# A table of buffers and a new order for the first 1550 steps of an attention and gated FFN kernel

## The chip, the cores and the metric

The kernel runs on one NeuronCore of a Trainium2 chip. The metric is the device time of one execution in microseconds (us), from several runs of the same kernel; a profile of one execution shows where that time goes. The names of the engines in the profile are PE (TensorE, with PEld for its weight loads), DVE (VectorE), ACT (ScalarE), POOL (GpSimd) and SP (SyncE, which issues most transfers).

## The reference

```python
def _attn_ref(q, k, v):                       # 8 batches, 8 heads, 576 rows, 64 columns
    q_s = softmax of q over its 64 columns
    k_s = softmax of k over the 576 rows
    kv = np.einsum('bhsd,bhse->bhde', k_s, v)
    return np.einsum('bhsd,bhde->bhse', q_s, kv)

def _moe_ref(x, w_gate, w_val, w_out, rms_g): # x: 4608 rows of 512, 1536 hidden columns
    rms = np.sqrt(np.mean(x * x, axis=-1, keepdims=True) + 1e-06)
    xn = x / rms * rms_g
    g = xn @ w_gate
    silu = g * (1.0 / (1.0 + np.exp(-g)))
    val = xn @ w_val
    return silu * val @ w_out
```

The heads of the attention's output are laid side by side and go as `x` into the gated FFN. The weights come as 64-bit floats.

## The kernel before, in words

The 4608 rows are nine blocks `j` of 512. Blocks 0 to 2 (`JP = 3`) go through the FFN one after the other; the other six are taken in three pairs `p`, for which the multiplications are saved by Strassen's scheme. The hidden columns are twelve chunks of 128. A step `s` counts block and chunk together: step 13 is chunk 1 of block 1.

The work is written as small functions, one per step. `ORDER` is a text of 3337 steps, which a loop at the end of the kernel calls from first to last under a manual schedule, so each engine receives its instructions in the order in which the text names them. A letter behind a colon chooses the engine: `:A` ScalarE, `:D` VectorE, `:P` GpSimd, `:S` the queue of SyncE. An engine takes its instructions strictly in turn and waits at the first that isn't ready.

The steps that matter here:

- `constants` makes the identity and `mean_w` on GpSimd; `warm` multiplies `mean_w` by itself on TensorE as filler (49 multiplications in all).
- K and V of a batch and a pair of heads: `k_load`, `k_max0` or `k_max` (maximum, VectorE), `k_tr` (transpose, TensorE), `k_top` (maximum, VectorE), `k_rows` (back, TensorE), `k_sub` (VectorE), `k_exp` (ScalarE), `k_mm` (K times V, TensorE), then `k_eps`, `k_rec` and `kv_hi`, `kv_lo` or `kv_norm0` (the normed product, split in two parts). `v_load` and `v_ones` fill V and its column of ones; `kv_zero` and `kv_zero0` clear buffers.
- q of a block and a pair of heads: `q_load`, `q_max`, `q_sub`, `q_exp`, `q_sum`, `q_rec`, `q_mul`, a transpose (`q_t`; for blocks 0 and 1 `q_t0` on TensorE with its copy `q_c0`), `q_hi` and `q_lo`, `q_x` or `q_x0` (q times KV, TensorE). Names that end in 0 are for the first blocks.
- x of a block: `x_hi`, `x_lo`, `x_sq`, then the norm in `n_sum`, `n_t`, `n_y0`, `n_y1`, `n_rows`.
- Weights: `load_w`, `conv_mul`, `conv_shift`, `conv_low` and `conv_add` turn 64-bit floats into 32-bit ones; `w_hi`, `w_lo`, `o_hi` and `o_lo` split a chunk into a rounded part and what is left (`copy` at L409 and the subtraction at L922 and L930); `s_add`, `s_hi`, `s_lo` do it for sums of weights that the pairs need, and `b_hi`, `b_lo`, `t_add` for the pairs' x.
- FFN of a step: `f1.s.0` and `f1.s.1` (gate and value, twelve 512-column multiplications each, L1005), `g_mul`, `silu`, `h_mul`, `h_hi` and `h_lo` (L1026), `f2` (twelve more, L1042) and at the end of a block `store`. For the pairs `pp` and later `qq` are TensorE's products.

Buffers come from pools with a number of places each, taken in turn. The eight PSUM banks are three pools: two for the results of `f1` (`ps_gv`), four for those of `f2` (`ps_o`), and two for all else (`ps_a`). The pairs choose among the pools by the table `BANKS`. A step that takes a bank waits until the last reader of the bank's former content is done: in `ps_gv` that is `g_mul` or `h_mul` of the step before.

Of the kernel before, what the change touches and what calls it, by code (L numbers as in the profile page):

```python
# [28 lines left out]
q_exp.0.2 q_eps0.0.0:D k_mm.0.0 k_eps.0.0:D conv_shift.1.1 warm.2.23 q_rec0.0.1 q_mul0.0.1:P conv_low.0.1.1 k_load.1.0
load_w.0.2 warm.2.11 q_rec0.0.0 k_sub.0.3 k_exp.0.3 k_rec.0.0 warm.2.12 q_sum0.0.2 q_eps0.0.2:A k_rows.0.2 k_sub.0.2  # L30
q_load0.1.0 v_ones.0.3 k_mm.0.1 k_eps.0.1:A conv_mul.0.1 warm.2.21 q_sub0.0.3:D load_w.2.1 k_rec.0.1 warm.2.22
q_rec0.0.2 q_exp.0.3 load_w.1.0 warm.2.5 k_mm.0.3 q_mul0.0.0:P q_t0.0.0 conv_mul.0.0 q_load0.1.1 load_w.3.0 load_w.2.0
q_mul0.0.2:P kv_norm0.0.0:D k_exp.0.2 k_eps.0.3:A q_t0.0.1 conv_low.0.0.1 kv_norm0.0.1:D conv_shift.0.1 conv_add.0.1.1
conv_shift.0.0 load_w.4.1 load_w.1.2 q_c0.0.0:A kv_zero0.1 q_sum0.0.3 q_eps0.0.3:D warm.2.13 q_rec0.0.3 q_c0.0.1:A
q_load0.1.2 k_mm.0.2 k_eps.0.2:A conv_mul.0.2 q_x0.0.0 k_max.1.0 conv_add.0.0.1 k_rec.0.3 kv_norm0.0.3:D warm.2.24
load_w.4.0 w_hi.0.0.2:A x_sq.0.0 k_tr.1.0 q_mul0.0.3:D q_t0.0.3 load_w.3.2 q_c0.0.3:A q_x0.0.1 k_rec.0.2 q_max0.1.0
# [1450 lines left out]
```

## Time and profile before

| what | value |
|---|---|
| device time, median of 3 runs | 932.93 us (932.87 to 935.09) |
| span of the profiled execution | 930.7 us |
| TensorE busy | 920.5 us (99%) |
| VectorE busy | 727.0 us (78%) |
| GpSimd busy | 522.4 us (56%) |
| ScalarE busy | 461.4 us (50%) |

The span runs from the first to the last instruction of the profiled execution and is its own time in the profile; the device time has 2.2 us around it that hold no instruction. A busy share is the part of the span in which an engine worked. A multiplication's recorded end is modelled, and neighbours overlap, so the pace of TensorE is better read from how long a whole group of multiplications takes.

### The profile page before, as it was taken

How to read it: one execution, taken by the hardware profiler on the slowest of the kernel's cores; microseconds unless marked ns; L12 is line 12 of the kernel's file. 1: busy time of each engine (PE TensorE's matmuls, PEld its weight loads, DVE VectorE, ACT ScalarE, POOL GpSimd, SP SyncE). 2: the span in 40 equal slices, each digit the busy share in tenths (PEclk: the TensorE clock that was granted, in tenths of full speed). 3: DMA queues.
4: the chain of work that ended last, by engine and by line, in shares of the span. 5: the costliest groups of instructions: out<-in, count | busy, mean ns of one | idle time of the engine just before them, and what ended most of it. 6: DMA issues, size and time to landing. Idle time of an engine off the chain costs nothing.

```text
span 930.7 us, 14213 instructions
## 1 busy us (share of the span) xinstructions
PE 920.5 (99%) x4621; PEld 748.1 (80%) x4621; DVE 727.0 (78%) x1520; ACT 461.4 (50%) x741; POOL 522.4 (56%) x539
## 2 busy tenths in 40 slices
...
GB/s 266 281 268 195 161 90 252 316 275 323 244 221 188 257 246 244 253 255 210 246 211 204 240 274 277 280 304 284 202 184 182 210 195 285 267 185 181 69 158 91
DMA packets 216569, 211.06 MB, mean 227 GB/s; under 512 B 138416, under 2 KB 177840, under 8 KB 211888
## 3 DMA queue, kind: packets, MB, share of 16 engines
...
q14 instruction: 36, 0.29, 0.1%
...
## 4 chain that ended last, share of the span: by engine, by line
PE 95%; DVE 3%; DMA 1%; issue 0%; ACT 0%; POOL 0%; DVEq 0%; ACTq 0%; POOLq 0%
PE ps_gv L1005 20%; PE ps_gv L1154 18%; PE ps_o L1154 12%; PE ps_o L1042 10%; PE ps_a L1154 7%; PE ps_o L1363 6%; PE ps_o L1247 4%; PE ps_a L1363 4%; PE ps_gv L1363 3%; PE ps_a L594 2%; PE ps_a L802 2%; PE ps_a L1247 2%; PE ps_gv L1247 2%; PE ps_o L802 1%; PE ps_gv L476 1%; DMA wd<-w 1%
## 5 line engine op out<-in xcount | busy, mean ns | idle before, releaser
L1005 PE MATMUL ps_gv<-xh,w 128*128 128x512 f32 x576 | 190.6, 397 | 1.3 <-DVE gs L1017 1.3
L1154 PE MATMUL ps_gv<-x,ring 128*128 128x512 f32 x576 | 143.0, 392 | 0.0
L1005 PEld LDWEIGHTS ps_gv<-xh,w 128*128 128x128 f32 x576 | 108.2, 188 | 26.0 <-DVE gs L1017 1.4
L1154 PEld LDWEIGHTS ps_gv<-x,ring 128*128 128x128 f32 x576 | 107.0, 188 | 23.0
L1005 PE MATMUL ps_gv<-xl,w 128*128 128x512 f32 x288 | 112.3, 391 | 0.0
L1175 DVE TENSOR_TENSOR tmp<-tmp,ps_gv 128x512 f32<-128x512 f32 x84 | 57.3, 684 | 49.6 <-PE ps_gv L1154 48.1
L1154 PE MATMUL ps_o<-x,ring 128*128 128x512 f32 x360 | 85.1, 389 | 0.0
L1127 POOL DMA_DIRECT2D ring<-wd x54 | 31.0, 575 | 91.3 <-PE ps_o L1154 34.1
L1154 PEld LDWEIGHTS ps_o<-x,ring 128*128 128x128 f32 x360 | 67.6, 188 | 14.2
L1042 PE MATMUL ps_o<-o,hh 128*128 128x512 f32 x288 | 73.1, 396 | 0.0
L1005 PEld LDWEIGHTS ps_gv<-xl,w 128*128 128x128 f32 x288 | 54.2, 188 | 10.6 <-issue 0.4
L1042 PEld LDWEIGHTS ps_o<-o,hh 128*128 128x128 f32 x288 | 53.0, 188 | 11.3 <-issue 0.4
L1175 DVE TENSOR_TENSOR tmp<-tmp,ps_o 128x512 f32<-128x512 f32 x42 | 28.7, 685 | 29.1 <-PE ps_o L1154 26.0
L409 ACT CAST hh<-gs 128x512 fp32r<-128x512 f32 x48 | 29.6, 616 | 31.7 <-DVE gs L1017 17.4
L1127 POOL DMA_DIRECT2D w<-wd x18 | 10.1, 559 | 58.2 <-PE ps_a L1154 37.9
L922 POOL TENSOR_TENSOR w<-w,w 128x512 fp32r<-128x512 f32 x29 | 39.3, 1363 | 5.1 <-ACT w L409 5.0
L1042 PE MATMUL ps_o<-o,hl 128*128 128x512 f32 x144 | 38.7, 391 | 0.0
L1154 PE MATMUL ps_a<-x,w 128*128 128x512 f32 x144 | 36.9, 392 | 0.0
L541 DVE TENSOR_REDUCE cm<-kt 128x128 f32<-128x640 f32 x28 | 36.7, 1310 | 0.1
L1154 PE MATMUL ps_a<-x,ring 128*128 128x512 f32 x144 | 36.7, 390 | 0.0
L1026 POOL TENSOR_TENSOR hl<-gs,hh 128x512 fp32r<-128x512 f32 x21 | 28.2, 1343 | 14.9 <-ACT hh L409 9.0
L1154 PE MATMUL ps_gv<-x,w 128*128 128x512 f32 x144 | 35.1, 391 | 0.0
...
## 6 DMA issues: line engine op xcount, KB each, us to landing
...
```

What stands on the lines that cost most here:

```text
L409: (e.copy if e is nc.scalar else e.tensor_copy)(dst, src)
L541: nc.vector.tensor_reduce(out=cm, in_=kt_[b, g].rearrange("p h j d -> p h d j"), axis=AX.X, op=ALU.max)
L802: nc.tensor.matmul(px[:, c0:c1], lhsT=wt, rhs=mv[:, c0:c1], start=(i == 0), stop=(i == 2))
L922: on(nc.gpsimd).tensor_tensor(out=w[:, :, 1], in0=halves(CHUNK[s], a, 1)[:, 0], in1=w[:, :, 0].bitcast(F32), op=ALU.subtract)
L1005: nc.tensor.matmul(pd[s], lhsT=w[:, a, c // 2, m, c % 2 * P:c % 2 * P + P], rhs=X[j, c][x], start=(n == 1), stop=(n == 3 * NKT))
L1026: on(nc.gpsimd).tensor_tensor(out=hl, in0=g_[s], in1=h_[s][0].bitcast(F32), op=ALU.subtract)
L1042: nc.tensor.matmul(po[t], lhsT=a[:, t * P:(t + 1) * P], rhs=w, start=(i == 0 and n == 0), stop=(i == NF - 1 and n == len(terms) - 1))
L1127: nc.gpsimd.dma_start(t, src.rearrange("p a b f -> p (a b f)"))
L1154: nc.tensor.matmul(abc[p, i, m, b], lhsT=src[:, h, c * P:(c + 1) * P], rhs=operand(o, c, x), start=first and n == 0, stop=n == 5, skip_gro ...
L1175: nc.vector.tensor_tensor(out=dst, in0=ux[u + (src,)], in1=abc[u + (b,)], op=ALU.add)
L1247: nc.tensor.matmul(pa[p, t, k], lhsT=a[:, k * P:(k + 1) * P], rhs=w, start=(c == 0 and n == 0), stop=(c == NF - 1 and n == 2))
L1363: nc.tensor.matmul(qacc[p, b, x], lhsT=ws[l][x], rhs=h[m], start=first and i == 0 and n == 0, stop=i == NH - 1 and n == 2, skip_group_chec ...
```

## The change

`ORDER` has the same 3337 steps in another order. In the sequence that each engine receives, the last difference stands at about step 1550, just ahead of the first product of the pairs (`pp.0.0.0.1`); from there on each engine has the same sequence as before. 181 steps have another engine letter, nearly all of them ahead of that place. From VectorE to GpSimd go, after those that go the other way are taken off, `w_lo` nine times, `s_lo` five and `o_lo` four times; from GpSimd to VectorE `q_mul`, `q_lo` and `x_nm`; from ScalarE to VectorE `h_hi`, `s_hi`, `b_hi`, some of `kv_hi`, `x_cp` and `q_c0`; to ScalarE from VectorE `kv_norm0` and `k_eps`.

The pools give way to a table, `SLOT`. It has a line for each kind of buffer: the width, and one digit for each time that the buffer is taken, in order, which names the place. The eight PSUM banks become one set (`ps.ps`, 390 digits), so any step can take any bank. A kind with width 0 still allocates a tile under the named place; one with a width uses one fixed tile for each place.

```diff
 ORDER = """
-kv_zero.4 k_load.0.0 v_ones.0.0 kv_zero0.0 g_load constants warm.2.2 warm.2.4 warm.2.7 warm.2.6 v_ones.1.1 k_max0.0.0
-warm.2.3 k_load.0.2 k_tr.0.0 k_top.0.0 k_max0.0.2 k_load.0.1 warm.2.8 k_max0.0.1 k_tr.0.2 warm.2.0 k_load.0.3
-k_max0.0.3 q_load0.0.1 q_max0.0.1 q_sub0.0.1:P q_exp.0.1 warm.2.1 k_rows.0.0 k_tr.0.3 warm.2.20 k_top.0.3 q_load0.0.2
-q_max0.0.2 v_ones.1.0 k_sub.0.0 k_exp.0.0 q_load0.0.0 v_load.0.0 k_tr.0.1 k_top.0.1 warm.9 warm.2.10 q_load0.0.3
-load_w.1.1 q_sub0.0.2:P q_max0.0.0 q_sum0.0.1 v_load.0.1 load_w.0.1 k_top.0.2 v_load.0.3 k_rows.0.3 load_w.0.0
-v_load.0.2 q_eps0.0.1:A q_sub0.0.0:P q_exp.0.0 conv_mul.1.1 q_max0.0.3 k_rows.0.1 k_sub.0.1 q_sum0.0.0 k_exp.0.1
...
-o_keep.12:S k_tr.2.1 store.0.0:A q_max2.2.2 n_rows.1 q_sub.2.2:P store.0.2:A k_top.2.1 g_mul.12 k_rows.2.1 s_lo.1.1:P
-k_mm.2.0 q_exp.2.2 k_sub.2.1 w_keep.13:S w_hi.14.0.2:A r_keep.1 f1.13.0 k_eps.2.0 q_half2.2.1 s_add.1.4:P k_load.2.2
-k_exp.2.1 q_max.2.3 silu.12 k_rec.2.0 w_lo.14.0:P k_mm.2.1 v_ones.2.2 w_lo.14.1:D kv_hi.2.0:A q_half.2.3 s_add.2.1:P
-s_keep.1.1:S v_load.2.2 store.0.3:A h_mul.12 s_add.0.1:P g_mul.13 f1.13.1 h_hi.12:A q_sum.2.2 h_lo.12:P kv_lo.2.0
-q_half2.2.2 s_add.0.3:P q_max2.2.3 q_sum2.2.2 q_sum2.2.1 k_eps.2.1 q_rec.2.2 k_rec.2.1 v_ones.2.3 q_sub.2.3:D
...
+v_ones.0.3 constants k_load.0.2 kv_zero.0 k_load.0.0 kv_zero.7 q_load0.0.1 kv_zero0.0 warm.2.7 k_load.0.1 warm.2.2
+k_load.0.3 q_load0.0.0 warm.2.6 k_max0.0.2 warm.2.4 load_w.0.1 k_max0.0.0 q_load0.0.2 warm.2.1 q_max0.0.1 v_load.0.1
+k_tr.0.0 q_sub0.0.1:D k_tr.0.2 v_load.0.0 k_top.0.0 q_exp.0.1 warm.2.10 k_max0.0.1 warm.2.8 k_max0.0.3 q_load0.0.3
+warm.2.20 q_sum0.0.1 warm.2.12 k_tr.0.3 load_w.1.1 q_max0.0.0 q_eps0.0.1:A warm.2.0 q_rec0.0.1 k_rows.0.0 k_top.0.3
+warm.2.3 q_sub0.0.0:P k_sub.0.0 k_tr.0.1 v_load.0.2 k_rows.0.3 warm.9 v_ones.0.0 q_mul0.0.1:P v_load.0.3 k_top.0.1
+k_exp.0.0 q_max0.0.2 load_w.0.0 q_exp.0.0 k_sub.0.3 q_sub0.0.2:P k_load.1.0 k_rows.0.1 k_top.0.2 warm.2.23 kv_zero.4
+q_exp.0.2 k_sub.0.1 warm.2.11 k_rows.0.2 k_mm.0.0 k_sub.0.2 k_exp.0.1 load_w.0.2 q_max0.0.3 conv_mul.0.1 q_load0.1.0
+k_mm.0.1 k_exp.0.3 q_sum0.0.0 q_sub0.0.3:P q_eps0.0.0:A k_exp.0.2 q_rec0.0.0 q_sum0.0.2 warm.2.5 conv_low.0.1.1
...
+s_lo.1.1:D h_hi.11:A k_exp.2.0 q_sum.2.2 h_lo.11:P s_keep.1.1:S k_tr.2.1 f2.10 q_half.2.3 o_keep.13:S q_lo.2.0:P
+n_y0.1 o_keep.12:S n_y1.1 s_add.1.4:P f2.11 q_max2.2.3 s_hi.1.4:A q_rec.2.1 q_sub.2.3:P k_top.2.1 n_rows.1 g_mul.12
+s_lo.1.4:P store.0.0:A s_add.2.1:D k_mm.2.0 w_hi.14.0.2:A s_lo.1.2:P k_rows.2.1 k_load.2.2 f1.13.0 s_hi.2.1:A
+k_sub.2.1 k_eps.2.0:A w_lo.14.0:D k_exp.2.1 kv_lo.1.2:P k_rec.2.0 store.0.3:A q_half2.2.2 s_add.0.1:P kv_hi.2.0:D
+k_mm.2.1 g_mul.13 kv_lo.1.3:P f1.13.1 kv_lo.1.1:P v_load.2.2 kv_lo.2.0 silu.12 q_mul.2.1:P store.0.1:A h_mul.12
+silu.13 v_ones.2.2 h_hi.12:D w_lo.14.1:D h_lo.12:P k_max.2.2 r_keep.5 store.0.2:A f2.12 w_hi.15.0.2:A q_sum2.2.2
...
+SLOT = """
+ap.kt 0 001011010101001010101010110101100110011001
+ap.qt 512 01202102102120102102102102021210120120
+fp.gs 512 2011202121021012101211201010121110221201201201201201201201200120120
+ps.ps 512 651637314556012451502136373164551247421662304457310652360314725765762756765627652765625726572657527652752676272765262572675260541762305023503025230230250235023503253505023506124735607417142172142174174127421741241214142741247414217144271453604217141414274142714412474142714427141724172472172400656503506630536053654136027563065306530653065306531721724721720647253172472172427127427127417260
+small.rs 1 01221011100102220102202102102102
+wsp.w 0 0111010101101010101010101010101010
...
+"""
+class Slots:
+    def __init__(self, pool, key):
+        self.pool, self.take, self.width, self.fixed = pool, {}, {}, {}
+        for line in SLOT.split("\n")[1:-1]:
+            tag, *rest = line.split()
+            if tag.startswith(key + "."):
+                tag = tag[len(key) + 1:]
+                self.width[tag], self.take[tag] = int(rest[0]), iter(rest[1])
+    def tile(self, shape, dtype, name, tag=None, bufs=None):
+        tag = tag or name
+        if tag not in self.take:
+            return self.pool.tile(shape, dtype, name=name, tag=tag, **({} if bufs is None else {"bufs": bufs}))
+        key = f"{tag}_{next(self.take[tag])}"
+        if not self.width[tag]:
+            return self.pool.tile(shape, dtype, name=name, tag=key, bufs=1)
+        if key not in self.fixed:
+            self.fixed[key] = self.pool.tile([128, self.width[tag]], F32, name=key, tag=key, bufs=1)
+        n = 1
+        for x in shape[1:]:
+            n *= x
+        t = self.fixed[key][:shape[0], :n]
+        if dtype is not F32:
+            t = t.bitcast(dtype)
+        axes = "abcd"[:len(shape) - 1]
+        if len(axes) > 1:
+            t = t.rearrange(f"p ({' '.join(axes)}) -> p {' '.join(axes)}", **dict(zip(axes, shape[1:])))
+        return t
...
-    wsp = ctx.enter_context(tc.tile_pool(name="wsp", bufs=2))
+    wsp = Slots(ctx.enter_context(tc.tile_pool(name="wsp", bufs=2)), "wsp")
     big = ctx.enter_context(tc.tile_pool(name="big", bufs=1))
-    xp = ctx.enter_context(tc.tile_pool(name="xp", bufs=8))
-    fp = ctx.enter_context(tc.tile_pool(name="fp", bufs=3))
-    ap = ctx.enter_context(tc.tile_pool(name="ap", bufs=2))
+    xp = Slots(ctx.enter_context(tc.tile_pool(name="xp", bufs=8)), "xp")
+    fp = Slots(ctx.enter_context(tc.tile_pool(name="fp", bufs=3)), "fp")
+    ap = Slots(ctx.enter_context(tc.tile_pool(name="ap", bufs=2)), "ap")
     kvp = ctx.enter_context(tc.tile_pool(name="kvp", bufs=8))
-    small = ctx.enter_context(tc.tile_pool(name="small", bufs=3))
-    ps_gv = ctx.enter_context(tc.tile_pool(name="ps_gv", bufs=NGV, space=PSUM))
-    ps_o = ctx.enter_context(tc.tile_pool(name="ps_o", bufs=T, space=PSUM))
-    ps_a = ctx.enter_context(tc.tile_pool(name="ps_a", bufs=8 - T - NGV, space=PSUM))
-    pools = {"a": ps_a, "v": ps_gv, "o": ps_o}
-    attn_pool = ["a"]
+    small = Slots(ctx.enter_context(tc.tile_pool(name="small", bufs=3)), "small")
+    psum = Slots(ctx.enter_context(tc.tile_pool(name="ps", bufs=8, space=PSUM)), "ps")
     turn = {}

-    def ps(role):
-        pool = {"attn": attn_pool[0], "gv": "v"}.get(role, role)
-        name = {"a": "ps_a", "v": "ps_gv", "o": "ps_o"}[pool]
-        return pools[pool].tile([P, TB], F32, name=name)
+    def ps():
+        return psum.tile([P, TB], F32, name="ps")
...
     def conv_mul(i, a):
-        cv[i, a] = ps("attn")
+        cv[i, a] = ps()
...
-    def attn_ps(first):
-        return ps("o" if first else "attn")
...
-            abc[p, i, m, b] = ps(BANKS[p % 2][0][b])
+            abc[p, i, m, b] = ps()
...
-            if t and p + 1 < NPAIR:
-                attn_pool[0] = BANKS[p % 2][1][3]
            for n in range(T):
-                pa[p, t, n] = ps(BANKS[p % 2][1 - t][n])
+                pa[p, t, n] = ps()
```

## Rows read from the trace of the kernel before

**Rows 1.** Page, part 1: engine, busy us (share of span), instructions

```profile
PE 920.5 (99%) x4621; PEld 748.1 (80%) x4621; DVE 727.0 (78%) x1520; ACT 461.4 (50%) x741; POOL 522.4 (56%) x539
```

**Rows 2.** Waits of TensorE in the whole span: us in total, times, longest

```profile
PE ps_gv L476 <- POOL vt L536: 2.3, 1, 2.3
PE ps_a L567 <- DVE kx L562: 1.4, 3, 0.7
PE ps_gv L1005 <- DVE gs L1017: 1.3, 1, 1.3
PE ps_o L711 <- DVE rs L618: 1.2, 1, 1.2
```

**Rows 3.** Windows: stretch, us, busy of PE, PEld, DVE, ACT, POOL; clock, DMA share, GB/s

```profile
0.00:36.00 36.00, 32.32 (x197) 22.26 (x198) 28.22 (x59) 21.60 (x39) 19.55 (x35) 1.00 1.02 284
36.00:300.00 264.00, 261.28 (x1407) 211.40 (x1406) 230.58 (x508) 191.99 (x295) 200.16 (x183) 1.00 0.75 232
300.00:368.00 68.00, 68.00 (x379) 55.75 (x378) 61.63 (x165) 46.53 (x72) 59.86 (x65) 1.00 0.95 253
```

**Rows 4.** Timeline of TensorE, start-up: start, length, instruction, idle before it

```profile
2.33 4.64 PE L476 MATMUL ps_gv<-mean_w 128*128 128x512 f32 x10 [2.33 <-POOL vt L536]
...
35.56 1.07 PE L1005 MATMUL ps_gv<-xh,w 128*128 128x512 f32 x4
```

**Rows 5.** Timeline of GpSimd, first microseconds

```profile
0.73 0.34 POOL L610 MEMSET kv<- 128x128 f32 x2 [0.29 <-POOLq L1472]
...
1.56 0.20 POOL masks.py:197 MEMSET ident<- 128x128 f32 x1
...
2.07 0.20 POOL L437 MEMSET mean_w<- 128x128 f32 x1
...
10.03 1.04 POOL L688 TENSOR_TENSOR qt<-qt,st 128x512 f32<-128x512 f32 x1 [7.44 <-DVE st L684]
```

**Rows 6.** Timeline of VectorE, start-up

```profile
3.85 0.55 DVE L547 TENSOR_TENSOR w<-w 96x384 f32<-96x384 f32 x1 [3.85 <-DMA w<-in_k_dram]
7.49 0.46 DVE L562 TENSOR_REDUCE kx<-ps_o 128x1 f32<-128x288 f32 x1 [3.08 <-PE ps_o L554]
...
9.26 0.68 DVE L684 TENSOR_REDUCE st<-qt 128x8 f32<-128x512 f32 x1
...
33.87 1.40 DVE L824 SCALAR_TENSOR_TENSOR xl<-ps_o,g_sb,xh 128x512 fp32r<-128x512 f32 x2
```

**Rows 7.** Timeline of ScalarE, its first row

```profile
8.63 1.28 ACT L751 ACT_TABLE_LOAD   x1 [8.63 <-DMA qt<-in_q_dram]
```

**Rows 8.** Timeline of all engines around the wait for a bank

```profile
152.07 0.80 DVE L573 TENSOR_TENSOR kt<-kt,ps_a 128x640 f32<-128x640 f32 x1
...
153.35 0.73 ACT L577 ACTIVATE kt<-kt 128x640 f32<-128x640 f32 x1
...
154.31 1.28 POOL L922 TENSOR_TENSOR w<-w,w 128x512 fp32r<-128x512 f32 x1
...
154.38 1.76 DVE L922 TENSOR_TENSOR w<-w,w 128x512 fp32r<-128x512 f32 x1
...
157.63 0.50 PE L1005 MATMUL ps_gv<-xh,w 128*128 128x512 f32 x1 [1.29 <-DVE gs L1017]
```

**Rows 9.** Timeline of TensorE around a transposed maximum

```profile
296.10 0.27 PE L557 MATMUL ps_a<-ident,cm 128*128 128x128 f32 x1
296.75 0.32 PE L567 MATMUL ps_a<-ident,kx 128*128 128x128 f32 x1 [0.39 <-DVE kx L562]
```

**Rows 10.** Instructions of line 922 until 370 us: ns min/median/max

```profile
L922 POOL TENSOR_TENSOR w<-w,w x29: 1267/1293/1750, 26.5 to 306.8; 128x512 fp32r<-128x512 f32 x29
L922 DVE TENSOR_TENSOR w<-w,w x23: 677/693/3921, 41.7 to 291.1; 128x512 fp32r<-128x512 f32 x23
```

**Rows 11.** Instructions of line 409 until 370 us, a cast on VectorE

```profile
L409 DVE CAST o<-w x4: 415/430/808, 74.9 to 141.0; 128x512 fp32r<-128x512 f32 x4
```

**Rows 12.** Chain that ended last, one piece: start, us, what

```profile
50.87 2.72 PE ps_gv L1005 x12
```

More of the change, by code (lines that the diff above doesn't have):

```diff
@@ L28 @@
-v_load.0.2 q_eps0.0.1:A q_sub0.0.0:P q_exp.0.0 conv_mul.1.1 q_max0.0.3 k_rows.0.1 k_sub.0.1 q_sum0.0.0 k_exp.0.1
[L29 to L36, printed above, removed]
-kv_norm0.0.2:D conv_low.0.2.1 conv_shift.0.2 q_t0.0.2 x_hi.0.0:A q_x0.0.3 k_top.1.0 k_rows.1.0 w_lo.0.0:P x_hi.0.1:D
@@ L138 @@
-q_sum2.4.1 q_max.4.3 q_x.4.0 q_half.4.3 n_hi.3:A k_mm.4.1 h_hi.26:A n_lo.3:D x_cp.4.0:A f1.27.1 o_lo.26:D v_ones.4.3
-q_exp.4.2 v_load.4.3 w_lo.28.1:D s_hi.4.4:A h_lo.26:D x_sq.4.0 k_eps.4.1 s_lo.4.4:P s_hi.5.4:A g_mul.27 q_rec.4.1
-f2.26 silu.27 k_rec.4.1 k_max.4.2 s_lo.5.4:P k_load.4.3 q_sum.4.2 q_mul.4.1:P kv_hi.4.1:A s_hi.5.3:A w_lo.28.0:P
-k_tr.4.2 k_top.4.2 s_keep.4.4:S o_hi.27:A q_half2.4.2 k_rows.4.2 s_keep.5.4:S f1.28.0 o_lo.27:P q_t.4.1 k_sub.4.2
-q_hi.4.1:A q_load.5.0 w_hi.29.0.2:A q_max2.4.3 h_mul.27 q_lo.4.1:P q_sum2.4.2 k_exp.4.2 q_rec.4.2 n_sum.3 kv_lo.4.1
@@ new lines @@
+q_t0.1.3 v_load.2.0 k_eps.1.3:A h_mul.10 q_c0.1.3:A h_lo.9:D f2.9 k_rec.1.3 conv_shift.11.2 kv_norm0.1.3:A w_keep.12:S
+w_lo.11.0:D conv_add.11.2.1 k_load.2.1 q_half2.2.1 q_x0.1.3 q_sum2.2.1 o_hi.10:D v_ones.2.0 f1.11.0 s_add.1.1:D
+x_sq.1.3 w_lo.11.1:D kv_hi.1.2:A kv_hi.1.3:D w_keep.13:S x_acc.1.3:D n_hi.1:A x_hi.1.3:A k_tr.2.0 n_lo.1:P f1.11.1
+k_top.2.0 o_hi.11:A g_mul.11 o_lo.10:D silu.11 o_lo.11:P s_hi.1.1:A x_lo.1.3 h_hi.10:A n_sum.1 q_half.2.2 k_rows.2.0
+f1.12.0 n_t.1 q_max2.2.2 h_mul.11 q_sub.2.2:P k_sub.2.0 s_add.1.2:P q_exp.2.2 k_max.2.1 f1.12.1 h_lo.10:P s_hi.1.2:A
@@ new lines @@
+q_load.3.0 h_hi.14:A w_hi.16.0.2:A w_lo.15.0:D k_mm.2.2 s_add.0.4:D q_x.2.1 o_hi.14:D h_lo.14:D o_lo.14:P f1.15.0
+k_max.2.3 x_hi.2.1:A o_keep.15:S k_eps.2.2:A w_keep.15:S k_rec.2.2 w_lo.16.0:P k_load.3.0 kv_hi.2.2:A kv_lo.2.2
+s_hi.0.1:A q_rec.2.3 w_lo.16.1:P s_hi.2.2:A q_t.2.2 k_tr.2.3 f1.15.1 x_sq.2.1 k_top.2.3 q_load.3.2 s_lo.0.1:D
+q_hi.2.2:A g_mul.15 q_lo.2.2:P q_max.3.0 f2.14 q_half.3.0 silu.15 v_ones.2.3 w_hi.17.0.2:A q_max2.3.0 x_lo.2.1
+q_sub.3.0:P k_max.3.0 x_acc.2.1:P q_x.2.2 h_mul.15 o_keep.14:S s_lo.2.2:D s_keep.0.1:S k_rows.2.3 k_tr.3.0 x_sq.2.2
```

609 lines of the change are left out of this document (315 added, 294 removed).

## The prediction

> **What bounds the kernel now.** I read the busy shares first. TensorE is busy 920.5 us [rows 1] of a span of 930.7, so at most about 10 us lie outside its work, and the change neither adds nor removes a matrix multiplication: both orders hold the same 3337 steps, the same 49 filler multiplications of `warm` among them. A group of twelve 512-column multiplications takes 2.72 us when nothing holds it [rows 12]; that is the pace that the new order has to keep, and it can't beat it.
>
> Next I read who TensorE waited for [rows 2]. The whole span has hardly more than this: 2.3 us before the first multiplication, 1.2 us in the start-up, 1.3 us once for a PSUM bank that `h_mul` had not yet read, and 1.4 us in three waits of `k_rows` for the column maximum of `k_top`. Together that is 6.2 us, and all of it lies before 300 us. The windows say the same from the other side: between 36 and 300 us TensorE lacks 2.7 us, between 300 and 368 it lacks nothing, although GpSimd is busy 59.86 of those 68 us [rows 3].
>
> Then I compared the two orders engine by engine. The last difference in any engine's own sequence stands at about step 1550, just ahead of the first Strassen product, `pp.0.0.0.1`, near 368 us in the trace. After that each engine has the same list in both, and only the buffers have other names. So the change can act on the first 368 us, by at most the 6.2 us of waits on the good side.
>
> **The change part by part.** *The first multiplication.* It waits for `mean_w`, which GpSimd fills in `constants`. Before it, GpSimd clears `kv_zero.4` and `kv_zero0.0` and sets one `v_ones`: from 0.73 to the start of `ident` at 1.56. From `ident` to the end of `mean_w` it is 1.56 to 2.27 [rows 5]. The new order has one `v_ones` and then `constants`, so `mean_w` should be ready at 0.73 + 0.1 + 0.71 = 1.54, and the fillers can begin 0.78 us sooner than at 2.33 [rows 4]. The two clearings are moved behind it; GpSimd has 7.4 us without work then [rows 5], which hides them.
>
> *The rest of the start-up.* TensorE reaches the first `f1` at 35.56 [rows 4], and VectorE works almost without a break from 7.49 to the end of the last `x_lo` at 35.3 [rows 6]. So VectorE has to come forward too, or the 0.78 us are given back in a later wait. It does: it stood still for 3.08 us until 7.49 because `k_top.0.0` is second in its list and TensorE needed until then [rows 6]. The new list has `k_max0.0.2`, `k_max0.0.0`, `q_max0.0.1` and `q_sub0.0.1` ahead of `k_top.0.0`, so a second `k_max0` (0.55) and a `q_max0` (0.68) fall into that gap. The first load lands at 3.85 [rows 6]. The q tile lands at 8.63 behind four K loads [rows 7]; in the new order two K loads and itself are 0.83 MB instead of 1.41, and between those two landings (0.29 MB by 3.85, 1.41 by 8.63) that gives about 6.2 us. So VectorE should have 1.2 us more done at 8 us. Over the block its load is about even: four `kv_norm0` go to ScalarE, three `q_c0` and one `w_hi` come from there. With that the 1.2 us wait of rows 2 (`q_t0` behind `k_rec`) has no cause left either. The gain of the start-up lies between 0 (all given back) and 0.78 + 1.2 = 2.0; I take 1.6, near the upper end, since the two engines that set its pace both start earlier.
>
> *The four waits between 150 and 300 us.* Two causes. In the first, `k_tr` is followed at once by `k_rows` on TensorE: at 296.10 and 296.75 nothing stands between them, and the wait is as long as the maximum that VectorE has to take [rows 9]. The new order has at least one other step between each such pair after 100 us, for instance `f2.10 f2.11 k_mm.2.0` between `k_tr.2.1` and `k_rows.2.1`, 5.4 us of cover by rows 12. In the second, `f1.13.1` waits 1.29 us for a bank that `h_mul.12` frees late, because the subtraction `w_lo.14.1` ahead of it on VectorE took 1.76 us while GpSimd, too, was at a subtraction [rows 8]; its median is 0.69 [rows 10]. In the new table `f1.13.1` takes bank 5, last read by `k_sub.2.1`. That step and the exponential behind it take 0.80 and 0.73 [rows 8] against 2.72 of `f1.13.0` ahead of it, so no wait is left there. Of 2.7 us I take 2.4 as won; the bounds are 0 and 2.7.
>
> *What moves between engines.* The new order takes `w_lo` from VectorE nine times, `s_lo` five and `o_lo` four times, and gives them to GpSimd: 18 subtractions of 1.29 instead of 0.69 us [rows 10]. From GpSimd go six `q_mul`, four `q_lo` and three `x_nm`, none above 1.3 us, so GpSimd gains at least 5 x 1.29 = 6.5 us, on 280 of 368 us [rows 3]. It stays below TensorE's 368. `h_hi` seven, `s_hi` five and `b_hi` four times go from ScalarE to VectorE, 0.43 us each [rows 11]; ScalarE becomes emptier by more than that. All of it is off TensorE's path as long as results come in time, so I cost it at nothing and put the risk into the next term.
>
> *New waits.* A new list of 1550 steps will have some of its own. The bounds are 0 and the 2.7 us that the present order has between 36 and 368 us; I take 0.9, a third of it, since cover between dependent steps is wider in the new list at the places I checked.
>
> *The buffers.* The table gives each PSUM and SBUF tile a fixed place; no instruction comes from it, only other waits. Behind 368 us I compared each PSUM place with its last reader: the products change between the same three or four banks as before, and TensorE waits nowhere there today, so nothing.
>
> Sum: -1.6 - 2.4 + 0.9 = -3.1 us. The profiled span 930.7 becomes 927.6. The median of the runs shown is 932.93, that is 2.2 us around the span, which stays: **929.8 us**.
>
> **The rivals.** *The start-up gives its gain back.* `v_load.0.0` and `v_load.0.1` stand behind one more weight load (512 KB) than before. If V lands late, `k_mm.0.0` waits, the fillers end too soon, and f1 begins where it did. For it: the DMA share is 1.02 in that stretch [rows 3], so every byte queued ahead counts. Against: VectorE was the pace there. Time: 932.9 - 2.4 + 0.9 = 931.4.
>
> *Collisions on VectorE.* Rows 8 show a VectorE subtraction of two SBUF tiles that ends 0.55 us after GpSimd's, and rows 10 a longest of 3.92 against 0.69; a cast there takes 0.43 us, and once 0.81 [rows 11]. The new order puts 16 more casts there and lengthens GpSimd's work, so there may be as many held instructions as before, at places that free banks: another 2.7 us of waits. Time: 932.9 - 1.6 - 2.4 + 2.7 = 931.6. The Trainium skill has this as a rule (GPSIMD Engine Reference, section Key points: GpSimd shares its SBUF interfaces with VectorE, and contends with VectorE instructions that have two SBUF inputs or use both ports); the rows above bear it out for both kinds.
>
> *GpSimd becomes late, and the kernel slower.* Between 300 and 368 us it has 8 us to spare [rows 3]. If the added subtractions push `h_lo` back, each `f2` there waits for it, up to 1.29 us each. The point from which it decides: the gains are 4.0 us and the bound for slower is 2.8 us, so six such waits or more. Against it: 13 other steps leave GpSimd, three `x_nm` of this very stretch among them. Time: 932.9 - 4.0 + 6 x 1.29 = 936.6.
>
> *Nothing moves.* The waits removed come back one for one in the next step, since VectorE and GpSimd are as full as before: 932.9.
>
> **How the numbers follow.** Less than 0.3% (2.8 us) can't be told from no change, so faster begins below 930.1. My forecast (929.8, its own range 928.1 to 931.0) has 0.54; start-up given back 0.17; collisions 0.12; nothing 0.08; late GpSimd 0.09. Some four fifths of the forecast's half lies below 930.1, with a little from the collisions: 0.46 faster, 0.45 the same, 0.09 slower. The best case is all waits gone and no new one: -2.0 - 2.7 = -4.7, 928.2, and the switch between small and large multiplications, 93 instead of 99 of them by the two lists, may add a few tenths: low end 927.9. The high end takes in the first two rivals and nothing moved: 932.9. Late GpSimd is left out.
>
> **What would show it.** The first multiplication at 1.5 to 1.6 us and the first `f1` of a chunk other than 0 some 2 us earlier; no wait of `k_rows` for `k_top` and none of `f1` for `h_mul` in TensorE's list; everything from the first `pp` to the end shifted by one amount, within 0.3 us. Wrong would be: a wait in the first 20 us on V or q loads, a wait of `f2` for `hl` on GpSimd, or any new wait behind 368 us, where I expect none.

## The result, and the profile after

The changed kernel takes 946.86 us (median of 4 runs, 946.25 to 948.79), the kernel before 933.51 in the same session: a ratio of 1.0149 (95% interval 1.0133 to 1.0164). The forecast was 929.8, its range up to 932.9. The profiled span is 945.6 us, 14.9 more than before. Runs of one kernel scatter, the kernel before from 932.2 to 941.6 us over all sessions and the version e7 below from 936.4 to 948.6, so small differences are read from profile rows here.

The start-up did what was forecast. The timeline of TensorE, its first row, answers to [rows 4]:

```profile
1.59 1.65 PE L534 MATMUL ps<-mean_w 128*128 128x512 f32 x3 [1.59 <-POOL mean_w L495]
```

f1.1.1, the first group behind the start-up, begins at 42.52 instead of 44.63 us (first the row of after, then that of before):

```profile
42.52 0.50 PE L1060 MATMUL ps<-xh,w 128*128 128x512 f32 x1
44.63 0.50 PE L1005 MATMUL ps_gv<-xh,w 128*128 128x512 f32 x1
```

The loss is further back. TensorE's waits in the whole span, the seven largest, columns as in [rows 2] (L1097 is now f2, L1060 f1, L1209 the pairs' products, L622 `k_rows`, L609 the first `k_tr`):

```profile
PE ps L1097 <- DMA o<-od: 4.3, 1, 4.3
PE ps L1097 <- DVE hl L1081: 4.1, 2, 3.0
PE ps L534 <- POOL mean_w L495: 1.6, 1, 1.6
PE ps L1209 <- DVE tmp L1230: 1.4, 1, 1.4
PE ps L622 <- DVE kx L617: 1.1, 1, 1.1
PE ps L609 <- DVE w L602: 1.0, 1, 1.0
PE ps L1097 <- DVE gs L1065: 0.6, 1, 0.6
```

The windows, columns as in [rows 3], and a fourth for where it hurts:

```profile
0.00:36.00 36.00, 32.78 (x206) 23.33 (x207) 28.15 (x58) 22.65 (x45) 21.00 (x36) 1.00 0.98 271
36.00:300.00 264.00, 259.83 (x1397) 209.39 (x1396) 235.33 (x509) 197.92 (x299) 211.64 (x189) 1.00 0.74 228
300.00:368.00 68.00, 63.35 (x345) 50.60 (x343) 56.61 (x141) 35.33 (x54) 53.22 (x59) 0.97 0.95 258
360.00:380.00 20.00, 12.74 (x39) 9.61 (x38) 8.29 (x24) 5.31 (x9) 5.90 (x6) 0.66 0.76 173
```

In the last window all engines stand: TensorE works 12.74 of 20 us, VectorE 8.29, GpSimd 5.90, while the granted clock is 0.66. The timeline of TensorE there:

```profile
359.77 0.61 PE L1060 MATMUL ps<-xh,w 128*128 128x512 f32 x2
364.67 3.75 PE L1097 MATMUL ps<-o,hh 128*128 128x512 f32 x8 [4.29 <-DMA o<-od]
371.40 1.22 PE L1097 MATMUL ps<-o,hl 128*128 128x512 f32 x2 [2.97 <-DVE hl L1081]
```

First f2.33 waits 4.29 us for the `w_out` chunk that `o_back.33` brings, then its third pass waits 2.97 us for `h_lo.33`. Behind each wait matmuls start every 427 ns instead of 227. From 360 to 378 us the starts of TensorE lie 12.3 us further apart than at its undisturbed pace (the sum is explained at the table below): 7.3 us are the two waits, 5.0 the slow stretches behind them. The chain of waits says what `h_lo.33` waited for:

```profile
356.16 13.87 DMA qt<-in_q_dram
370.02 0.04 issue
370.06 0.69 DVE st L785
370.75 0.61 DVE hl L1081
371.35 0.04 issue
371.40 2.07 PE ps L1097 x4
```

Not for its inputs: it stands on VectorE behind `q_max.6.1` (`st`, L785), and that waits 9.98 us for q. The last piece of `q_load.6.1`, issued at 353.97, took 15.87 us and landed at 369.84; the chain names the piece that landed next, at 370.02. Both waits end in a transfer. What was in front of them is in GpSimd's timeline, its transfer rows alone (L1016 `o_back`, L1012 `w_back`, L1182 `w_in`, L1194 `o_in`):

```profile
343.81 0.60 POOL L1016 DMA_DIRECT2D o<-od  x1
344.41 0.71 POOL L1012 DMA_DIRECT2D w<-wd  x1
345.10 0.59 POOL L1182 DMA_DIRECT2D ring<-wd  x1
346.69 0.62 POOL L1194 DMA_DIRECT2D ring<-od  x1
347.30 0.55 POOL L1182 DMA_DIRECT2D ring<-wd  x1
349.16 0.57 POOL L1194 DMA_DIRECT2D x<-od  x1
353.65 0.57 POOL L1182 DMA_DIRECT2D ring<-wd  x1
355.36 0.53 POOL L1016 DMA_DIRECT2D o<-od  x1 [1.15 <-PE ps L1097]
355.88 0.71 POOL L1012 DMA_DIRECT2D w<-wd  x1
358.56 0.57 POOL L1016 DMA_DIRECT2D o<-od  x1
```

and the same of the kernel before (L961 `o_back`, L957 `w_back`, L1127 `w_in`, L1139 `o_in`):

```profile
337.04 0.59 POOL L961 DMA_DIRECT2D o<-od  x1
342.49 0.78 POOL L957 DMA_DIRECT2D w<-wd  x1 [1.14 <-PE ps_gv L1005]
345.07 0.59 POOL L961 DMA_DIRECT2D o<-od  x1 [0.16 <-issue]
351.63 0.77 POOL L957 DMA_DIRECT2D w<-wd  x1 [2.40 <-PE ps_gv L1005]
352.39 0.55 POOL L1127 DMA_DIRECT2D ring<-wd  x1
355.45 0.57 POOL L1127 DMA_DIRECT2D ring<-wd  x1
356.01 0.54 POOL L961 DMA_DIRECT2D o<-od  x1
356.53 0.55 POOL L1139 DMA_DIRECT2D x<-od  x1
```

Before, one `w_back` stands between `o_back.32` and `o_back.33`, which leaves at 345.07. After, five transfers of the pairs' weights (3.7 MB, first used at 382 us in this trace) stand there as well, and `o_back.33` leaves at 355.36. Before, two of the five had left at 310.34 and 320.25 us, and three leave behind 352 us. In its new place `o_back.33` could hardly leave sooner: the table gives it the buffer that `o_back.32` had, and it waits 1.15 us until f2.32 has read it. Transfers by queue between 344 and 370 us after (q0 GpSimd's, q1 SP's; packets, MB, share of 16 engines' time):

```profile
q0 software_dynamic: 1696, 7.34, 82.9%
q1 hardware_dynamic: 3808, 0.46, 30.5%
```

To see where the 14.9 us are, I summed TensorE's starts by stretch: for each two neighbouring multiplications the distance of their starts, less the tenth percentile for such a pair of shapes in the same trace (the floor). The sum takes in waits and half-rate stretches alike ("over the floor", us):

| kernel | 0-50 | 50-175 | 175-350 | 350-400 | 600-650 |
|---|---|---|---|---|---|
| before | 14.8 | 10.1 | 10.7 | 2.2 | 0.2 |
| after | 13.5 | 8.0 | 16.0 | 14.8 | 1.9 |

With the 0.74 us by which the first multiplication is earlier, the start-up gains 2.0, the waits at 151 to 158 us another 2.1; the new order loses 5.3 up to 350 us, 12.6 at 350 to 400, and 1.7 near 640. (The floors of the two traces differ by 1.1 us as well.)

### The profile page after: what moved, and what is told of

Same layout as the page of the kernel before. It is cut to its first block, busy times and chain, and to the rows that moved or that the text cites. A ratio compares the mean times of both kernels' runs of the same rounds, so it can differ in the third digit from the quotient of the medians.

```text
span 945.6 us, 14168 instructions
## 1 busy us (share of the span) xinstructions
PE 925.2 (98%) x4621; PEld 750.1 (79%) x4621; DVE 735.3 (78%) x1523; ACT 461.4 (49%) x740; POOL 535.1 (57%) x545
## 4 chain that ended last, share of the span: by engine, by line
PE 75%; DVE 11%; DMA 8%; SPq 2%; issue 2%; ACT 1%; POOL 0%; DVEq 0%; POOLq 0%; ACTq 0%
PE ps L1209 35%; PE ps L1416 12%; PE ps L1060 11%; PE ps L1300 7%; PE ps L1097 5%; DMA qt<-in_q_dram 2%; PE ps L857 2%; PE ps L649 1%; SPq L719 1%; DMA raw<-in_moe_w_out_dram 1%; DVE gs L1065 1%; DMA sd<-kt 1%; DMA w<-in_v_dram 1%; DVE gs L1072 1%; DMA kt<-in_k_dram 1%
## 5 line engine op out<-in xcount | busy, mean ns | idle before, releaser
L1209 PE MATMUL ps<-x,ring 128*128 128x512 f32 x1080 | 257.9, 391 | 1.4 <-DVE tmp L1230 1.4
L1209 PEld LDWEIGHTS ps<-x,ring 128*128 128x128 f32 x1080 | 201.5, 188 | 44.6 <-DVE tmp L1230 1.9
L1060 PE MATMUL ps<-xh,w 128*128 128x512 f32 x576 | 189.5, 399 | 0.6 <-DVE gs L1065 0.4
L1230 DVE TENSOR_TENSOR tmp<-tmp,ps 128x512 f32<-128x512 f32 x126 | 85.9, 685 | 77.2 <-PE ps L1209 72.3
L1060 PEld LDWEIGHTS ps<-xh,w 128*128 128x128 f32 x576 | 108.9, 189 | 26.6 <-issue 0.7
L1060 PE MATMUL ps<-xl,w 128*128 128x512 f32 x288 | 112.2, 393 | 0.0
L1209 PE MATMUL ps<-x,w 128*128 128x512 f32 x432 | 102.2, 391 | 0.0
L1209 PEld LDWEIGHTS ps<-x,w 128*128 128x128 f32 x432 | 80.6, 188 | 17.1
L1182 POOL DMA_DIRECT2D ring<-wd x54 | 31.1, 575 | 93.1 <-PE ps L1209 88.1
L1097 PE MATMUL ps<-o,hh 128*128 128x512 f32 x288 | 75.8, 405 | 5.6 <-DMA o<-od 4.3
L1097 PEld LDWEIGHTS ps<-o,hh 128*128 128x128 f32 x288 | 53.7, 192 | 19.2 <-issue 5.4
L1060 PEld LDWEIGHTS ps<-xl,w 128*128 128x128 f32 x288 | 54.6, 190 | 10.8 <-issue 0.4
L1097 PE MATMUL ps<-o,hl 128*128 128x512 f32 x144 | 39.8, 399 | 4.3 <-DVE hl L1081 4.1
L1182 POOL DMA_DIRECT2D w<-wd x18 | 10.1, 560 | 58.2 <-PE ps L1209 58.2
L1097 PEld LDWEIGHTS ps<-o,hl 128*128 128x128 f32 x144 | 27.3, 191 | 11.5 <-DVE hl L1081 5.2
```

The lines of the kernel that those rows point to most:

```text
L1060: nc.tensor.matmul(pd[s], lhsT=w[:, a, c // 2, m, c % 2 * P:c % 2 * P + P], rhs=X[j, c][x], start=(n == 1), stop=(n == 3 * NKT))
L1097: nc.tensor.matmul(po[t], lhsT=a[:, t * P:(t + 1) * P], rhs=w, start=(i == 0 and n == 0), stop=(i == NF - 1 and n == len(terms) - 1))
L1182: nc.gpsimd.dma_start(t, src.rearrange("p a b f -> p (a b f)"))
L1209: nc.tensor.matmul(abc[p, i, m, b], lhsT=src[:, h, c * P:(c + 1) * P], rhs=operand(o, c, x), start=first and n == 0, stop=n == 5, skip_gro ...
L1230: nc.vector.tensor_tensor(out=dst, in0=ux[u + (src,)], in1=abc[u + (b,)], op=ALU.add)
```

## The experiments

Theory A: the transfers on GpSimd's queue jam (more is queued than lands in time), and hold up `o_back.33` and SP's small pieces alike. Rivals: B, the shared buffer; C, the place of `h_lo.33` on VectorE; D, `q_load.6.1`, which is issued later than before, is the root. (The texts below put that at 334 us before; the trace has `q_load.5.3` there, and `q_load.6.1` from 340.97 on, so it is 3.7 us later.) Every time below is a median; the ratio to the kernel before of the same session stands beside it, with its 95% interval. Rows and sums are of the one profiled run, which lay 3 to 4 us under the median for e4 (940.7) and e7 (936.4) and 3 us above it for e5 (941.7), e12 (950.8) and e16 (941.3).

**One cause taken away at a time.** In the changed kernel, on GpSimd, on VectorE, and all at once (of GpSimd's steps the transfers alone are shown):

```diff
 # e1_own_buffer: the last five digits of wsp.o complemented
-w_back.34 w_in.0.0.0.2 o_in.0.0.0 w_in.0.0.0.1 o_in.0.0.1 w_in.0.0.1.2 o_back.33 w_back.35 o_back.34
+w_back.34 o_back.33 w_in.0.0.0.2 o_in.0.0.0 w_in.0.0.0.1 o_in.0.0.1 w_in.0.0.1.2 w_back.35 o_back.34
 # e2_five_behind: buffers as they are
+w_back.34 o_back.33 w_back.35 o_back.34 w_in.0.0.0.2 o_in.0.0.0 w_in.0.0.0.1 o_in.0.0.1 w_in.0.0.1.2
 # e3_hlo_ahead
-q_max.6.1 h_lo.33:D
+h_lo.33:D q_max.6.1
 # e4_all_three: e1, e2 and e3
```

> Edit to the changed kernel: o_back.33 stands ahead of w_in.0.0.0.2 and takes the other of the two wsp.o buffers (the one that f2.31 freed), and the four tiles after it change places in the same way. Theory A (a jam of transfers): the ten transfers that GpSimd issues between 343.8 and 358.6 us (7.2 MB) hold up everything behind them, o_back.33 and the small pieces of q_load.6.1 alike. Then the wait for o_back.33 (4.29 us at 364.67) goes, but q_load.6.1 still lands at about 370, VectorE still stands at q_max.6.1 until then with h_lo.33 behind it, and the third pass of f2.33 starts at about 371 as before: 945 to 947 us, one wait of some 7 to 8 us in place of 4.29 and 2.97. Theory B (the shared buffer): o_back.33 was late because its buffer was the one that f2.32 still read; with its own it is in time, and 4.3 us and part of the half-rate stretch come back: 939 to 943 us. Theory C (order on VectorE): as A, the second wait stays, but for h_lo.33's place alone: 943 to 946 us.

Measured 945.0 (1.0126, interval 1.0111 to 1.0141). That is A's forecast. One wait of 8.1 us took the place of two:

```profile
PE ps L1097 <- DVE hl L1081: 8.1, 1, 8.1
```

> Edit to the changed kernel: w_in.0.0.0.2, o_in.0.0.0, w_in.0.0.0.1, o_in.0.0.1 and w_in.0.0.1.2 (3.6 MB, needed only by pp.0.0.0 behind 374 us) stand behind o_back.34; buffers as they are. Theory A (jam): o_back.33 still leaves at about 355.4, since its buffer frees then, but with little ahead of it it lands at 359 to 361; q_load.6.1 lands before 358 and h_lo.33 is in time. Both waits shrink to less than 1.5 us together and the half-rate stretch goes: 935 to 939 us. Theory B (shared buffer): the issue at 355.4 is what is late, so the first wait keeps 2 us or more, and the second wait has nothing to do with it: 941 to 946 us. Theory C (order on VectorE): the second wait stays until h_lo.33 is moved: 940 to 943 us.

Measured 941.57 (1.0092, 1.0070 to 1.0115). Both waits of f2.33 are gone, so B and C fail, but the time is above A's range too: new ones came, 1.1 us of f2.32 for `h_lo` on GpSimd at 355 us, and two behind the same transfers at their new place, for `v_load` (named `tmp`, L649 is `k_mm`) and for a `w_in`:

```profile
PE ps L649 <- ACT tmp L467: 2.0, 1, 2.0
PE ps L1209 <- DMA ring<-wd: 1.1, 1, 1.1
```

The first of these two rows is named after ScalarE, which had long been done; the chain of waits has `vt<-in_v_dram`, 15.34 us from 363.57, in its place.

> Edit to the changed kernel: h_lo.33 stands ahead of q_max.6.1 on VectorE and nothing else. All theories: the wait of 2.97 us at 371.40 goes, the one of 4.29 us at 364.67 stays. Theory A (jam): VectorE still stands at q_max.6.1 until about 370, so a part of the 2.97 us turns up at the next thing that PE wants from VectorE (k_tr.5.2, g_mul and h_mul of chunk 34): 942 to 945 us. Theory C (order on VectorE is the fault): the whole 2.97 us and half of the half-rate stretch come back: 940 to 942 us.

Measured 947.3 (1.0141, 1.0122 to 1.0159): the wait of 2.97 us turned into 4.48 us of `k_tr.5.2` for VectorE. C is out; A had the move of the wait, but not its size.

> The three edits together: o_back.33 ahead with its own buffer, the five transfers behind o_back.34, h_lo.33 ahead of q_max.6.1. Theory A: both waits and the half-rate stretch (12.6 us over the floor between 350 and 400 us in the changed kernel against 1 to 2 before) go, and nothing of it comes back behind: 933 to 937 us; about the same as with the five transfers behind alone, or up to 2 us less. A rival that all of A, B and C miss: the wait only moves on, because the five transfers are then late for pp.0.0.0 or the next loads: 938 us or more, with new waits at 375 to 400 us.

Measured 944.44 (1.0133, 1.0107 to 1.0159), with a scatter of 940.7 to 948.7. 9.2 us stay over the floor at 350 to 400 us: the rival that A, B and C miss. Waits of 2.0 and 1.8 us come for VectorE; the second follows a K piece that fills 11.92 us of the chain of waits. Moving the load away from f2.33 moves the jam on.

**The old order of the transfers, and the casts.** e5 puts the ten transfers of this stretch back into the old sequence, but for two: `w_in.0.0.0.2` and `o_in.0.0.0` leave at 336 us in it, while the kernel before issued them at 320 and 310 (the text below takes their old place to be 333). e6 returns 28 casts and copies from VectorE to ScalarE; e8 does the reverse of e5, in the kernel before:

```diff
 # e5_old_transfers (changed kernel, last five digits of wsp.o complemented)
+o_back.31 w_in.0.0.0.2 o_in.0.0.0 ... w_back.34 o_back.33 ... w_back.35 w_in.0.0.0.1 w_in.0.0.1.2 ... o_back.34 o_in.0.0.1
 # e6_casts_back (28 such)
-h_hi.21:D
+h_hi.21:A
 # e8_before_jam (kernel before)
-o_back.33
+w_in.0.0.0.2 o_in.0.0.0 w_in.0.0.0.1 o_in.0.0.1 w_in.0.0.1.2 o_back.33
```

> The changed kernel with GpSimd's transfers of this stretch in the order of the kernel before: w_in.0.0.0.2 and o_in.0.0.0 go back behind o_back.31 (about 333 us), o_back.33 back behind w_back.34 with the free wsp.o buffer, then w_back.35, w_in.0.0.0.1, w_in.0.0.1.2, o_back.34, o_in.0.0.1. Nothing else is touched. Theory A (a jam: what GpSimd has queued holds up SP's small pieces, whichever tile they are for): with 1.3 MB gone from the stretch behind 344 us, o_back.33 and q_load.6.1 (still issued at about 344) land by 357, and the waits of 2.0 to 2.1 us that the run with the five behind still had for v_load and k_load shrink: 935 to 939 us, 0 to 3 us over the floor of the kernel before between 350 and 400 us. Theory D (the late q_load.6.1, issued at 344.6 instead of 334 us, is the root, and any order of the rest meets it): a wait of 2 us or more stays at 355 to 380 us: 939 to 942 us.

Measured 938.69 (1.0064, 1.0041 to 1.0088): 8 us back, inside A's range. In the profiled run 7.1 us over the floor stay at 350 to 400 us (1.5 us of `q_x` for `k_sub`, which VectorE reaches late because a K piece lands at 374.4; 1.3 and 0.3 us of f2 for `h_lo`). Whether that is the rest of the order or the two transfers that still leave 16 and 26 us later than before isn't told apart.

> The kernel before with one part of the change alone: w_in.0.0.0.2, o_in.0.0.0, w_in.0.0.0.1, o_in.0.0.1 and w_in.0.0.1.2 stand ahead of o_back.33 on GpSimd, as in the changed kernel. Buffers and all else as before. Theory A (the jam alone is enough): o_back.33 lands at about 358 to 362 us instead of 351.4, and the pieces of q_load.6.2 and the k and v loads behind 345 us land 5 to 10 us later: a wait of 2 to 6 us on PE at 355 to 375 us, 936 to 941 us. Theory D (it takes the late q_load.6.1 as well): q_load.6.1 has landed by 344.6 us here, ahead of the jam, and o_back.33 lands just in time: 932 to 935 us.

Measured 945.51 (1.0131, 1.0116 to 1.0146). Five steps moved in the old order, with old buffers and old engines, cost 12 us, more than A gave it:

```profile
PE ps_o L1042 <- DVE hl L1026: 8.4, 2, 7.7
PE ps_o L1042 <- DMA o<-od: 0.7, 1, 0.7
```

`q_load.6.1` leaves at 340.57 here and has landed by 354.3, so D is out: the next load, `q_load.6.2`, was caught instead (pieces of 346 to 349 us landed 13 to 19 us later), and VectorE, with `h_lo.33` in its queue behind `q_max.6.2`, stood 9.99 us for it (the row names the K piece that landed next):

```profile
367.25 0.69 DVE L730 TENSOR_REDUCE st<-qt 128x16 f32<-128x512 f32 x1 [9.99 <-DMA kt<-in_k_dram]
```

> The changed kernel with 28 steps that it moved from ScalarE to VectorE behind f1 of chunk 12 (h_hi 6, s_hi 5, b_hi 4, kv_hi 4, x_cp 4, o_hi 2, q_hi, x_hi, n_hi 1 each) back on ScalarE, at the same places of the order. Theory E (VectorE is too full): between 175 and 350 us VectorE is busy 162.5 us in the changed kernel and 155.1 before, and the new waits there (0.28, 0.34, 0.41, 1.13, 0.34, 1.08, 0.60 us) end nearly all on VectorE; with some 8 to 12 us less work on it they shrink by half or more: 2 to 4 us less than the changed kernel between 175 and 300 us, 942 to 945 us in all, with the waits at 364 and 371 us left. Rival F (the order of steps on VectorE makes the waits, not its load): the waits stay within 1 us of what they were, or ScalarE becomes what is late: 946 to 949 us.

Measured 947.12 (1.0149, 1.0133 to 1.0164). The window from 175 to 350 us, first of the changed kernel, then of e6:

```profile
175.00:350.00 175.00, 170.67 (x935) 137.48 (x934) 162.53 (x381) 104.88 (x162) 135.06 (x130) 1.00 0.78 235
```

```profile
175.00:350.00 175.00, 169.24 (x929) 136.39 (x928) 150.33 (x349) 117.40 (x187) 134.09 (x130) 1.00 0.78 235
```

VectorE has 12.2 us less to do and TensorE lacks no less. The waits that end on VectorE halve, from 3.8 to 2.0 us (those for `hl`, 1.1, and `gs`, 0.6, stayed; that of `k_rows` for `k_top` went), and 3.2 us of new ones came for ScalarE, two for `hh` and one for `kv`:

```profile
PE ps L1097 <- ACT hh L467: 2.2, 2, 1.3
PE ps L857 <- ACT kv L472: 1.0, 1, 1.0
```

So the move gives nothing back, as rival F has it (ScalarE becomes what is late). That VectorE's load has no part in the waits isn't shown.

> Both edits together. Theories A and E: the two gains add, since they lie in different stretches (175 to 300 us and 350 to 400 us): 932 to 936 us, which would be as good as the kernel before or a little better. If they don't add, one of the stretches hands its wait to the next: 937 us or more.

Measured 940.64 (1.0075, 1.0051 to 1.0099), scattered from 936.4 to 948.6: at 350 to 400 us the profiled run, the fastest, has 4.7 over the floor, at 175 to 350 us 17.4. The second edit still gives nothing in its own stretch.

**The order cut in two.** The same steps exist in both orders, so a first part of one can be followed by the rest of the other, each step with the engine letter that it has there. (The lines of e9, e13 and e14 have numbers one higher than those of the changed kernel.) The table is worked out anew for such an order: each tile takes the place that has been free longest.

```diff
 # e9: first 740 steps new, rest old          # e10: first 740 old, rest new
 # e11: all old                               # e12: all new
-SLOT of the changed kernel
+SLOT worked out for that order
 # e13: as e9, tiles first used in the first 740 steps keep their old digits
 # e14: first 1340 steps new with their own digits, rest old
```

> The code of the changed kernel (buffers named by a table, eight PSUM banks as one set) with an order in two parts: the first 740 steps in the new order (to about 165 us), all others in the order of the kernel before; the table is worked out anew for it, each tile taking the free buffer that has been free longest. Theory G (the parts of the change have signs of their own, and the order behind 175 us is what costs): the start-up gain (f1.1.1 at 42.5 instead of 44.7 us) and the waits of 0.75 and 1.29 us at 151 to 158 us that went are kept, nothing else is paid: 928 to 930 us, faster than before by 0.3 to 0.5%. Rival H (what the start-up gains is taken back by the next stage, since engines behind it are no earlier): 932 to 934 us. Rival I (the buffers or the one set of banks cost, wherever the order comes from): 935 us or more.

Measured 931.52 (0.9970, 0.9950 to 0.9989): a little faster than before, by less than G's forecast; H is out by the ratio, and two waits at 80 us (0.79 and 0.45) come from the table that I worked out or from the meeting of the orders.

> The reverse: the first 740 steps in the old order, the rest in the new one, table worked out in the same way. Theory G: it keeps the slow start and the waits at 151 to 158 us and takes all of the loss behind: the 946.9 us of the changed kernel and 4 us, 949 to 952 us. Rival H (the loss comes from the new first part, whose engines reach 175 us in another state): 940 us or less.

Measured 958.66 (1.0261, 1.0240 to 1.0282). That is above G's figure by what e11 shows: two waits for L524 (`conv_shift`) near 58 and 77 us come from the table that I worked out. G keeps the rest: 16.3 over the floor at 175 to 350 us and 12.5 at 350 to 400, as in the changed kernel.

> The old order throughout in the code of the changed kernel, table worked out in the same way: the buffers and the set of eight PSUM banks alone. Theory G: they're worth nothing by themselves, since places of PSUM or SBUF hold almost nothing up in the kernel before: 932 to 934 us. Rival I: slower by 2 us or more.

Measured 945.07 (1.0113, 1.0085 to 1.0142), against G. Most of it is in the first 80 us, in two waits for `conv_shift` at 58 and 78 us:

```profile
PE ps L1060 <- DVE w L524: 6.7, 2, 3.7
```

and from 175 to 400 us it is near the kernel before (11.4 and 3.7 over the floor against 10.7 and 2.2). So buffers can cost 11 us, though that is this table's fault, and the changed kernel has no such wait.

> The new order throughout, with the table worked out in the same way in place of the one that came with it. o_back.33 then has the buffer that f2.31 freed, but stands as late on GpSimd as before, behind five other transfers. Theory A (the jam of transfers is what costs at 364 to 378 us, and it is a matter of order): 944 to 948 us. Theory B (the table that came with the order is at fault): 940 us or less.

Measured 947.61 (1.0134, 1.0107 to 1.0161): with other buffers throughout, the new order has three of the waits at 230 to 265 us at the same steps (1.48, 0.33 and 1.05 us, instead of 1.13, 0.34 and 1.08) and the jam too (2.76 us for `o_back.33`, 3.98 for `h_lo.33`). They belong to the order. A wait of 4.0 us for `h_lo` at 79 us is this table's.

> As the version new then old (first 740 steps in the new order, the rest in the old one), but tiles of the first 740 steps keep the places of the changed kernel's own table; only those behind are worked out anew. Theory G: the waits of 0.79 and 0.45 us at 80 us came from the table worked out anew and go: 929 to 931 us, faster than before by 0.3 to 0.5%. Rival: they come from the meeting of the two orders and stay: 931 to 932 us.

Measured 931.02 (0.9960, 0.9933 to 0.9987), profiled span 928.2. This is the best version: new start, old rest. The waits of 0.79 and 0.45 us at 80 us went, others of 0.56 and 0.38 us came at 106 and 114 us.

> The new order for the first 1340 steps (to about 310 us) with its own places, the old order behind, so that GpSimd's transfers from 344 us on stand as in the kernel before. Theory A and G: of the changed kernel's 946.9 us the 12.6 us over the floor at 350 to 400 us go and the new waits at 175 to 280 us (some 5 us) stay: 933 to 936 us. Rival: the transfers still meet, because what stands ahead of them is in the new order: 939 us or more.

Measured 943.01 (1.0079, 1.0051 to 1.0107), a miss: 2.6 over the floor at 350 to 400 us, the waits at 236 to 280 us kept (1.10, 0.34, 1.06, 0.58), but 4.4 us of new waits of `k_mm` (L650) where the orders meet, at 321 and 340 us:

```profile
PE ps L650 <- issue: 3.0, 1, 3.0
PE ps L650 <- ACT kt L633: 2.0, 2, 1.4
```

The chain of waits goes through `vt<-in_v_dram` from 324.42, 6.49 us, behind GpSimd's 1.6 MB of 318 and 319 us.

**A single letter, and the banks.**

```diff
 # e15_h_lo19_on_gpsimd (changed kernel)
-h_lo.19:D
+h_lo.19
 # e16_old_order_old_banks: e11 with ps.ps in three sets of banks
```

> The changed kernel with h_lo.19 on GpSimd as in the kernel before, instead of VectorE, where it stands behind q_mul.3.1 (1.64 us) and o_lo.20 (0.96 us), both also moved there by the change. The wait of 1.13 us at 233.49 us goes by every theory. Theory F (single steps in the wrong queue make these waits one by one): nothing takes its place up to 262 us, and the span falls by about 1.1 us but for the scatter: 944.5 to 946.5 us. Rival: VectorE and GpSimd are so full here that the next step takes the wait over (f2.20 at 242 us waits 1 us more): 946 to 948 us.

Measured 951.01 (1.0177, 1.0125 to 1.0229). The wait went from 1.13 to 2.34 us: GpSimd came to the step later than VectorE had. Another wait of 1.7 us at 81 us and the usual jam are in that trace too, so the whole 4 us isn't this letter's. Both theories missed.

> The old order throughout in the code of the changed kernel as in the run with the old order and new buffers, but its PSUM tiles keep to the three sets of banks of the kernel before (two, four and two); SBUF places are the same as in that run. If the one set of eight banks made the two waits of 3.7 and 2.9 us for conv_shift at 58 and 78 us: 932 to 935 us. If SBUF places made them: 942 us or more.

In this version `conv_mul.3.1` takes the bank of `q_t0.1.0` before `q_c0.1.0` has read it, so that part of block 1 is computed from overwritten values. Measured 938.22 (1.0037, 1.0005 to 1.0069), between the two forecasts. The waits for `conv_shift` shrank from 6.7 to 2.5 us (now `q_x0` has it, at 58 us), so the banks seem to have had most of them, but with that overlap it isn't settled.

## Why the prediction was wrong

- *The first multiplication and the start-up* were right: 1.59 us (1.54 forecast), f1.1.1 2.1 us earlier against 1.6 taken (bound 2.0). The q tile landed at 6.51 us (about 6.2 forecast). One of its signs of being wrong did show, 0.49 us of `k_mm` for V at 19.43 us, but f1 did not begin later for it. That the gain is given back in the next stage fell with e9 and e13, which keep it to the end.
- *The four waits between 150 and 300 us* went at their places, also right. But `k_rows` has another wait for `k_top`, 1.08 us at 263.6, which the prediction excluded. The cover on TensorE was there, a whole f2 from 259.51 on; `k_top` was late because VectorE, behind other steps in its list (a cast among them that took 1.20 instead of 0.42 us), came to it at 263.29 only.
- *What moves between engines, at nothing.* Not settled. Giving 28 casts and copies back to ScalarE gains nothing (e6), but the other letters were only tried together with the order, and the one tried by itself made its wait longer (e15). GpSimd's busy time grew by 12.7 us in the whole span, from 522.4 to 535.1, against "at least 6.5" (five `q_mul` leave it, not six).
- *New waits, 0.9 us with bounds 0 and 2.7.* This is the step that failed, in two ways; the runs show 5.3 us up to 350 us and 12.6 behind in its place. The upper bound was read from the few waits of the old order; a new order has no such bound, and the stretch from 175 to 350 us alone went from 10.7 to 16.0. And "the places I checked" were pairs of dependent steps on the engines; the transfers that moved steps issue on GpSimd's queue were never put in a row. Moving five of them so costs 12 us in the kernel before (e8), and moving them back gives 8 of the 13.4 us back in the changed one (e5).
- *The buffers, nothing.* Their wait behind 368 us, 1.45 us for `tmp` at 640.24, did come. VectorE stands 4.47 us there for `vt<-rd`. But e3 has no such wait with the same order and places behind 368 us, e1, e2 and e4 have 0.7 to 1.6 us, and e8 and e9 have 0.7 and 1.2 us with the old order there: so neither order nor table decides it alone. VectorE's wait for a transfer suggests that it goes with how transfers fall; what decides it is open.
- *Late GpSimd* was the rival on the right side (936.6), with the wrong mechanism: `h_lo.33` on VectorE was late for a q load, not on GpSimd for its subtractions.
- *The low end of the range* takes in a few tenths for six switches fewer between small and large multiplications. No row of this case prices a switch; the floors of the two traces, which hold them all, differ by 1.1 us.

Open: which steps of the new order make the 5 us of waits between 175 and 350 us. The table that came with it isn't needed for them (e12), and the order with its letters is shown as a whole (e9, e10, e13).

The rival *Collisions on VectorE*, priced at 2.7 us, is not out. Take for each VectorE instruction between 175 and 350 us its length less the median for its operation and shape in the same trace: the sum is 11.7 us before and 17.8 after, and e6, with 12 us less work on VectorE, still has 17.4. An estimate for one wait: ahead of the 1.13 us for `h_lo.19`, VectorE works without a break from 227.91 to 233.44, and `q_mul` takes 1.64 us, `o_lo` 0.96 and `h_lo` 1.44 instead of 0.69 each, 2.0 us in all, beside GpSimd at work. But the sum alone doesn't decide: e7 and e8 have 14.5 and 14.7 us of it, and 17.4 and 10.7 over the floor. No run varied it.
